# Engine order given by the kernel's own step planner, second-layer weights prepared behind the first batch's heads, transform tables in four transfers

## The chip, the cores and the metric

One Trainium2 chip, one of its cores. The metric is device time of one execution in microseconds (us). The engines are named as the profile names them: PE (TensorE matmul), PEld (its weight loads), DVE (VectorE), ACT (ScalarE), POOL (GpSimd) and SP (SyncE, which here only issues transfers).

## The reference

Attention over 8 batches x 8 heads (576 positions, 64 channels a head, block-causal mask), then a Fourier mixing of each batch, a normalization and a feed-forward layer with residual:

```python
scores = np.where(mask, scale * np.matmul(q, k.transpose(0, 1, 3, 2)), -1000000000.0)
attn = softmax(scores)
x = np.matmul(attn, v)                      # per head, then heads side by side: (8, 576, 512)
u = x + np.real(fft(fft(x, axis=1), axis=2))
un = (u - mean(u)) / np.sqrt(var(u) + 1e-06)
out = u + np.maximum(un @ w_ch1, 0.0) @ w_ch2     # 512 -> 2048 -> 512
```

The two weight matrices arrive as float64, 8.4 MB each.

## The kernel before, in words

The work is cut into small steps. Each step is a `Step` (line 137): a function that records instructions, its cost on PE, a chain of costs on the other engines (D for DVE, A for ACT, G for POOL, Q for SP), the steps it comes after, and a place in the sequence. Lanes yield steps in order: the loads of a head (`head_lane`), its split into a leading part and a rest (`prepare_lane`: `lead` on ACT L293, `rest` on DVE L308 and POOL L310, with two copies L301/L302), the values (`v_lane`, L323 to L340), the row maxima (`max_part`, L388 to L394), their transposed shift (`shift`, L403, and the small copy `lead<-mt`, L405), the scores with two exponentials and a difference (`scores`, ACT L434/L435, POOL L436), the products with the values (`values`, PE into `av`, DVE L471 to L474) and, once per batch, the transform (`fourier_steps`: `mirror`, `folded`, two stages of matmuls, then `normalized_steps`).

The main loop at the end of the kernel walks a model of time. At each turn it picks the step that is ready first, records all of its instructions at once (`step.emit()` in `issue`) and books its chain on queues of the other engines. The feed-forward layer of 256 rows (a "filler", `feed_steps`; 18 of them in all) is taken where no lane is ready. PE keeps the order in which the steps are recorded (`keep_in_program_order`, lines 194 and 197). The order on DVE, ACT, POOL and SP is not given by the kernel: the framework's scheduler sorts those instructions by a time model of its own.

The weights are a side lane, `weight_lane`. Every float64 pair is turned into float32 by three DVE operations over 128x1024 words (`weight_single`, L836 to L838) and one ACT square that sums the magnitude (L839); this is done for 14 pairs of 128-row blocks and 4 single blocks, the first layer's 8 pairs, then the second layer's 6 pairs and 4 singles. Then each of the 32 blocks is scaled and split into two f16 parts (`weight_parts`: ACT L863 and L866 with POOL L867 for the first layer, ACT L863 and DVE L869 for the second). The loads go out on SP's queue (L826), up to three ahead. Heads of the second batch start only when all 18 loads are converted ("w32"). The tables of the transform (2606 KB) come in one transfer on POOL's queue after head 4 (L910).

## Time and profile before

| | us |
|---|---|
| median of 3 runs | 1315.61 (1313.72 to 1317.63) |
| the profiled execution, its own time | 1315.5 |
| its span in the trace | 1313.7 |
| PE busy | 1184.2 |
| DVE busy | 671.9 |
| ACT busy | 548.5 |
| POOL busy | 530.0 |

In the lines of the profile `out<-in` names the tile written and the tiles read, `x14` the number of instructions, and L836 the line of the kernel. A row that groups instructions gives busy time and the mean of one in ns, then the idle time of the engine just before them and what ended it. A row of a window gives the busy us of each engine in that stretch, the clock that PE was granted (1.00 is full), and the share of the transfer engines. "SPq" and "ACTq" are transfers being issued by that engine. A tile's PSUM buffer shows as ps, h or acc whichever ring it was taken from, so those names alone do not tell the step.

### The profile page before, as it was taken

How to read it: one execution, taken by the hardware profiler on the slowest of the kernel's cores; microseconds unless marked ns; L12 is line 12 of the kernel's file. 1: busy time of each engine (PE TensorE's matmuls, PEld its weight loads, DVE VectorE, ACT ScalarE, POOL GpSimd, SP SyncE). 2: the span in 40 equal slices, each digit the busy share in tenths (PEclk: the TensorE clock that was granted, in tenths of full speed). 3: DMA queues.
4: the chain of work that ended last, by engine and by line, in shares of the span. 5: the costliest groups of instructions: out<-in, count | busy, mean ns of one | idle time of the engine just before them, and what ended most of it. 6: DMA issues, size and time to landing. Idle time of an engine off the chain costs nothing.

```text
span 1313.7 us, 25264 instructions
## 1 busy us (share of the span) xinstructions
PE 1184.2 (90%) x10068; PEld 886.7 (67%) x10068; DVE 671.9 (51%) x1440; ACT 548.5 (42%) x1137; POOL 530.0 (40%) x578
## 2 busy tenths in 40 slices
PE   3464469999898999999999999999899999999998
PEld 2363357777676777677777777777677767767665
DVE  6983776445645564655546544746372432412211
ACT  3569355545354444444545354544543112111110
POOL 4668143444544553455443645436442500300000
PEclk9955679999699999999999999999999999999999
DMA  9756213232223223322242133223211000000000
GB/s 280 230 175 177 93 29 77 84 106 64 61 65 92 76 50 90 93 76 51 80 115 75 44 96 104 73 70 86 79 30 49 30 12 17 22 1 17 16 17 17
DMA packets 55941, 99.10 MB, mean 75 GB/s; under 512 B 7709, under 2 KB 26605, under 8 KB 55696
## 3 DMA queue, kind: packets, MB, share of 16 engines
q1 hardware_dynamic: 52176, 87.56, 23.5%
q0 software_dynamic: 2288, 7.54, 1.9%
q10 hardware_dynamic: 1360, 2.38, 0.6%
q8 instruction: 80, 1.31, 0.4%
q14 instruction: 37, 0.30, 0.1%
HBM read 58.46 MB, written 18.87 MB: 59 GB/s over the span
## 4 chain that ended last, share of the span: by engine, by line
PE 76%; DVE 10%; ACT 4%; DMA 3%; POOL 3%; issue 3%; SPq 0%; ACTq 0%; DVEq 0%; POOLq 0%
PE h L194 27%; PE acc L194 26%; PE ps L194 16%; PE av L194 5%; POOL pl L436 2%; PE ps L197 1%; DVE M L392 1%; DVE W L837 1%; DMA W<-in_moe_w_ch_dram 1%; DVE rest L308 1%; DVE W L838 1%; ACT lead L293 1%; DVE tmp L549 1%; DMA U<-xd,rows 1%; DVE W L836 1%
## 5 line engine op out<-in xcount | busy, mean ns | idle before, releaser
L194 PE MATMUL h<-uh,W 128*128 128x256 f16 x2304 | 434.9, 275 | 0.0
L436 POOL TENSOR_TENSOR pl<-p,ph 128x288 f16<-128x288 f32 (+1 forms) x256 | 257.9, 1017 | 395.8 <-ACT p L435 249.6
L194 PEld LDWEIGHTS <-W 128*128 128x128 f16 x3456 | 325.8, 99 | 64.3 <-issue 4.0
L194 PE MATMUL acc<-W,gh 128*128 128x512 f16 x1152 | 347.2, 383 | 0.0
L194 PE MATMUL h<-ul,W 128*128 128x256 f16 x1152 | 316.2, 274 | 0.0
L194 PE MATMUL acc<-W,gl 128*128 128x512 f16 x576 | 220.1, 382 | 0.4 <-DVE gl L750 0.4
L750 DVE SCALAR_TENSOR_TENSOR gl<-h,gh 128x512 f16<-128x512 f32 x144 | 98.9, 687 | 227.3 <-ACT gh L749 227.2
L194 PE MATMUL ps<-lead 72*128 72x64 f32 (+9 forms) x700 | 196.5, 342 | 12.5 <-ACT lead L293 6.8
L749 ACT ACTIVATE gh<-h 128x512 f16<-128x512 f32 x144 | 85.9, 596 | 268.4 <-PE h L194 267.7
L434 ACT ACTIVATE ph<-ps 128x512 f16<-128x512 f32 (+1 forms) x229 | 116.0, 507 | 121.0 <-PE ps L194 119.7
L194 PEld LDWEIGHTS <-gh 128*128 128x128 f16 x1152 | 101.0, 99 | 87.8 <-issue 8.2
L392 DVE TENSOR_REDUCE M<-ps 128x1 f32<-128x320 f32 (+3 forms) x235 | 120.5, 527 | 47.9 <-PE ps L194 46.7
L194 PE MATMUL av<-VH,pl 128*128 128x65 f16 x960 | 115.9, 200 | 31.7 <-POOL pl L436 31.5
L194 PEld LDWEIGHTS ps<-lead 72*128 72x128 f32 (+1 forms) x700 | 125.6, 201 | 20.8 <-ACT lead L293 6.8
L194 PEld LDWEIGHTS <-ph 128*128 128x128 f16 x1920 | 113.0, 103 | 34.1 <-DVE x L474 8.4
L310 POOL TENSOR_TENSOR rest<-raw,lead 64x576 fp32r<-64x576 f32 x64 | 116.2, 1816 | 23.3 <-ACT lead L293 18.5
L194 PE MATMUL av<-VH,ph 128*128 128x65 f16 x960 | 118.1, 202 | 8.2 <-DVE x L474 7.6
L194 PE MATMUL ps<-rest 128*128 128x64 f32 (+2 forms) x345 | 121.6, 360 | 1.8 <-DVE M L392 1.1
L435 ACT ACTIVATE p<-ps 128x512 f32<-128x512 f32 (+1 forms) x229 | 115.9, 506 | 10.2 <-POOL pl L436 10.1
L194 PE MATMUL av<-VL,ph 128*128 128x64 f16 x960 | 117.3, 200 | 0.0
L194 PEld LDWEIGHTS <-pl 128*128 128x128 f16 x960 | 93.6, 102 | 34.9 <-POOL pl L436 34.8
L308 DVE TENSOR_TENSOR rest<-raw,lead 64x576 fp32r<-64x576 f32 x64 | 60.0, 938 | 88.4 <-ACT lead L293 88.3
(171 smaller groups left out, 1376.7 us busy)
## 6 DMA issues: line engine op xcount, KB each, us to landing
raw<-in_qk_dram SPq DMA_DIRECT2D x64, 288.0 KB
rest<-lead SPq DMA_DIRECT2D x112, 144.0 KB
W<-in_moe_w_ch_dram SPq DMA_DIRECT2D x14, 1024.0 KB
V<-in_v_dram SPq DMA_DIRECT2D x32, 320.0 KB
xd<-x SPq DMA_DIRECT2D x32, 256.0 KB
out_dram<-u SPq DMA_DIRECT2D x32, 256.0 KB
u<-xd SPq DMA_DIRECT2D x8, 512.0 KB
dft<-in_c_dft_dram POOLq DMA_DIRECT2D x1, 2606.0 KB, 11.3
```

The source lines that it names most:

```text
L194: return tc.keep_in_program_order(nc.tensor.matmul(*args, **kw))
L197: return tc.keep_in_program_order(nc.tensor.transpose(*args, **kw))
L293: nc.scalar.copy(LEAD[h % NB][0:D, 64:], raws[h])
L308: nc.vector.tensor_tensor(x0[0:D, 0:S], raw[:, 0:S], x1[0:D, 64:64 + S], op=ALU.subtract)
L310: nc.gpsimd.tensor_tensor(x0[D:P, S:], raw[:, S:], x1[0:D, 64 + S:], op=ALU.subtract)
L392: nc.vector.tensor_reduce(m[:, j:j + 1], t[:, at - hi:at], axis=AX.X, op=ALU.max)
L434: nc.scalar.activation(ph[:, at:at + w], t[:, 0:w], AF.Exp, scale=0.125)
L435: nc.scalar.activation(p32[:, 0:w], t[:, 0:w], AF.Exp, scale=0.125)
L436: nc.gpsimd.tensor_tensor(pl[:, at:at + w], p32[:, 0:w], ph[:, at:at + w], op=ALU.subtract)
L549: nc.vector.tensor_tensor(e[0:r], X[c][0:r], U[c][0:r], op=op)
L749: nc.scalar.activation(gh, t, AF.Relu)
L750: nc.vector.scalar_tensor_tensor(gl, t, 0.0, gh, op0=ALU.max, op1=ALU.subtract)
```

## The change

1. **Order.** A class `Ordered` wraps DVE, ACT, POOL and SP so that all their instructions keep the order in which the kernel records them. A step no longer records everything at once: its function has become a generator with a `yield` behind the part of each engine. `issue` books the chain, notes a start time for each part, and `give` records the parts whose planned start has come before the next PE step is recorded. The planner's model gains queues for the port that DVE and POOL share (K) and for transfers (M), and rings for three scratch tiles.
2. **Weights.** The loads form a lane of their own and go out on ACT's queue; the first two also wait for the first V and the first two heads. Two further lanes prepare the layers: the second layer's conversions come after head 7's values and after the first layer's scale. Heads of the second batch wait for the last f16 part of the first layer instead of for all 18 conversions. The first layer's f16 parts start after its scale step, which stood on PE behind the scores of head 5 and now stands inside the first batch's transform.
3. **Tables.** Four transfers instead of one, after heads 1, 2, 4 and 5, each behind a one-element DVE operation.
4. **Smaller edits.** For the first batch the copies of `lead_copies` and `shift` move from ACT's queue to SP's, as for the other batches before. The last maximum (L394) becomes a `tensor_scalar` with the second operand as a per-partition scalar. In the first batch's transform the 12 additions of stage 2 move from DVE to POOL, as in the other batches. Several `need` conditions (recorded before) become `after` conditions (done before, in the model).

The core of the diff:

```diff
+class Ordered:
+    def __getattr__(self, name):
+        f = getattr(self.engine, name)
+        def given(*args, **kw):
+            x = f(*args, **kw)
+            return self.tc.keep_in_program_order(x) if hasattr(x, "ins") else x
+        return given
...
+    def give(t):
+        soon = sorted((x for x in pending if x[0] <= t), key=lambda x: x[:2])
+        pending[:] = [x for x in pending if x[0] > t]
+        for _, _, parts in soon:
+            next(parts, None)
...
-            nc.vector.tensor_tensor(m[:, 4:5], m[:, 4:5], m[:, 5:6], op=ALU.max)
+            vector.tensor_scalar(m[:, 4:5], m[:, 4:5], m[:, 5:6], None, op0=ALU.max)
...
-            engine = nc.vector if b == 0 else nc.gpsimd
+            engine = gpsimd
...
-            nc.sync.dma_start(raw(x).rearrange("p (j n) -> p j n", j=n), weight(i, n))
+        if x < 2:
+            vector.tensor_copy(raw(x)[0:1, 0:1].bitcast(F32), raws[x][0:1, 0:1])
+            yield
+        scalar.dma_start(raw(x).rearrange("p (j n) -> p j n", j=n), weight(i, n))
...
+                    (("WL", x),) + ((("WS", x - 1),) if x else ()) + ((("scale", 0), ('V', 7, 4)) if w else ()), ("WS", x),
...
-        nc.vector.tensor_scalar(dft[0:1, 0:1], DEN[0][0:1, 0:1], 0.0, None, op0=ALU.mult)
-        nc.gpsimd.dma_start(dft, c_dft)
+        vector.tensor_scalar(dft[0:1, lo:lo + 1], DEN[i % 2][0:1, 0:1], 0.0, None, op0=ALU.mult)
+        yield
+        gpsimd.dma_start(dft[:, lo:hi], c_dft[:, lo:hi])
...
-            if x is not None and may(x) and (i == len(lanes) - 1 or x.place < H or "w32" in done)
+            if x is not None and may(x) and (i == len(lanes) - 1 or x.place < H or ('w', 15) in done)
```

What this does to the order is shown at three places. In the changed kernel every instruction of DVE, ACT, POOL and SP carries line 194, that of `given`.

DVE between the end of head 0 and the end of head 1 (`x<-av` is a head's last DVE operation, `W<-W` the conversion of weights, `M` the maxima, `rest` the split of a coming head). Before, the first 12 of 30 rows:

```order
L474 TENSOR_TENSOR x<-av,rec 128x5x64
L836 TENSOR_SCALAR W<-W 128x1024
L337 TENSOR_SCALAR vacc<-pw 128x1
L837 SCALAR_TENSOR_TENSOR W<-W 128x1024
L838 SCALAR_TENSOR_TENSOR W<-W 128x1024
L392 TENSOR_REDUCE M_91<-ps 128x1 x2
L836 TENSOR_SCALAR W<-W 128x1024
L392 TENSOR_REDUCE M_91<-h 128x1
L340 SCALAR_TENSOR_TENSOR VL_97<-V,vacc,VH_95 128x640
L837 SCALAR_TENSOR_TENSOR W<-W 128x1024
L308 TENSOR_TENSOR rest_88<-raw,lead_85 64x576
L394 TENSOR_TENSOR M_91<-M_91 128x1
```

Now, all rows of that stretch:

```order
L194 TENSOR_TENSOR x<-av,rec 128x5x64
L194 TENSOR_REDUCE M_91<-h 128x2
L194 TENSOR_REDUCE M_91<-h 128x1
L194 TENSOR_TENSOR rest_87<-raw,lead_84 64x576
L194 SCALAR_TENSOR_TENSOR VL_97<-V,vacc,VH_95 128x640
L194 TENSOR_REDUCE M_91<-acc 128x1 x2
L194 TENSOR_REDUCE M_91<-ps 128x1
L194 TENSOR_SCALAR M_91<-M_91 128x1
L194 TENSOR_TENSOR rest_88<-raw,lead_85 64x576
L194 TENSOR_SCALAR DEN_93<-av,vacc 128x5
L194 RECIPROCAL rec<-DEN_93 128x5
L194 TENSOR_TENSOR x<-av,rec 128x5x64
```

No conversion stands there any more. Counted over the whole order, all 14 pairs stood ahead of head 7's `x<-av` before and 6 do now; the other 8 stand between it and the first normalization of the transform, and the 4 singles, which stood among the transform's first operations, come behind that normalization.

ACT in the first batch's transform (`ZT`, `fs` and `zs` are the transform's tiles, `W<-W,wst` and `un<-W,wst` the f16 parts of the first layer, `left,ul<-W` the square of a converted pair). Now:

```order
L194 CAST ZT<-ps 2x290
L194 ACTIVATE left,ul<-W 128x1024
L194 DMA W<-in_moe_w_ch_dram 128x2x1024
L194 CAST fs_1294<-tmp 32x256 x2
L194 CAST fs_1298<-tmp 128x256
L194 CAST fs_1312<-tmp 128x256
L194 ACTIVATE W<-W,wst 128x512
L194 ACTIVATE un<-W,wst 128x512
L194 CAST zs_1335<-h 128x288
L194 ACTIVATE W<-W,wst 128x512
```

Before, those parts began among the exponentials (`ph`, `p`) of head 6:

```order
L435 ACTIVATE p_899<-ps 128x512
L434 ACTIVATE ph_960<-h 128x288
L863 ACTIVATE W<-W,wst 128x512
L866 ACTIVATE un<-W,wst 128x512
L863 ACTIVATE W<-W,wst 128x512
L435 ACTIVATE p_965<-h 128x288
L866 ACTIVATE un<-W,wst 128x512
L434 ACTIVATE ph_960<-h 128x288
```

So the first layer's f16 parts move from the last two heads of the batch to the middle of its transform, and a load of weights stands in ACT's order ahead of casts.

SP at the start of the program (`raw` a head's q and k, `V` the values of two heads, `rest<-lead` and `lead<-mt` the copies that a head waits for). Before:

```order
L290 DMA raw<-in_qk_dram 64x1152
L314 DMA V<-in_v_dram 128x640
L290 DMA raw<-in_qk_dram 64x1152
L826 DMA W<-in_moe_w_ch_dram 128x2x1024 x4
L290 DMA raw<-in_qk_dram 64x1152 x2
L826 DMA W<-in_moe_w_ch_dram 128x2x1024
L314 DMA V<-in_v_dram 128x640
```

Now:

```order
L194 DMA raw<-in_qk_dram 64x1152
L194 DMA V<-in_v_dram 128x640
L194 DMA raw<-in_qk_dram 64x1152
L194 DMA rest_87<-lead_84 64x576 x2
L194 DMA raw<-in_qk_dram 64x1152
L194 DMA rest_88<-lead_85 64x576 x2
L194 DMA lead_84<-mt 1x5x128
```

The weights are gone from SP's order; the copies of the first batch have come into it.

More of the change, by code (lines that the diff above doesn't have):

```diff
@@ L247, in tile_attn_fourier_ffn @@
     now = 0.0
-    queues = {x: Queue() for x in "DAGQ"}
+    queues = {x: Queue() for x in "DAGQKM"}
     done = {}
@@ L259, in ready, with book @@
         return max(r, min(rings[x][0] for x in lent)) if step.bank else r
+    def book(engine, t, cost):
+        used = [queues[x] for x in {"X": "DK", "G": "GK", "P": "G"}.get(engine, engine)]
+        while True:
+            at = max(x.fit(t, cost) for x in used)
+            if at <= t:
+                return max(x.book(t, cost) for x in used)
+            t = at
+    pending = []
+    issued = [0]
     def issue(step):
@@ L263, in issue @@
         t = max(now, ready(step))
+        if step.cost:
+            give(t)
         if step.cost:
@@ L268, in issue @@
         free = None
+        starts = []
         for engine, cost in step.chain:
@@ L500, in max_lane @@
                 )
[L501 removed]
+            yield Step(lambda: shift(h), 0.12, ("A0.26", "B", "Q0.6", "M0.05", "L1.6"), (("M", h),), ("X", h), True, place=h - 0.6)
     def value_lane():
@@ L934, in tile_attn_fourier_ffn @@
         until = max(now, min(until, default=now))
-        if side is not None and may(side) and ready(side) <= until:
-            engine, cost = side.chain[0] if side.chain else (None, 0.0)
+        first = min((heads[i].place for i in able), default=H) >= H
+        for w, side in enumerate(sides):
+            if side is None or not may(side) or ready(side) > until:
+                continue
+            engine, cost = next((x for x in side.chain if x[0] in "DAGQKXP"), (None, 0.0))
             at = max(now, ready(side))
-            ahead = queues[engine].fit(at, cost) - at if engine else 0.0
-            first = min((heads[i].place for i in able), default=H) >= H
-            if ahead <= AHEAD[engine == "D" and first] or at + ahead + cost + FREE <= until:
+            ahead = queues[{"X": "D", "P": "G"}.get(engine, engine)].fit(at, cost) - at if engine else 0.0
+            if ahead <= AHEAD[engine in ("D", "X") and first] or at + ahead + cost + FREE <= until:
                 issue(side)
-                side = next(weights, None)
-                continue
+                sides[w] = next(weights[w], None)
+                break
+        else:
+            w = None
+        if w is not None:
+            continue
         feed = filler is not None and may(filler)
@@ L952, in tile_attn_fourier_ffn @@
             i = min(able, key=lambda i: ready(heads[i]))
-        elif side is not None:
-            issue(side)
-            side = next(weights, None)
+        elif any(sides):
+            w = min((w for w, x in enumerate(sides) if x is not None and may(x)), key=lambda w: ready(sides[w]))
+            issue(sides[w])
+            sides[w] = next(weights[w], None)
+            continue
+        elif pending:
+            give(pending[0][0])
             continue
```

385 lines of the change are left out of this document (230 added, 155 removed).

## The prediction, made before the changed kernel was run

> **What bounds the kernel now.** I read the page first, then windows by stage, then who PE waits for, and last the chain of waits in the stage where PE stands idle. The page gives the span, the engines, PE in 40 slices of 32.8 us and the clock granted to it:
>
> ```profile
> span 1313.7 us, 25264 instructions
> PE   3464469999898999999999999999899999999998
> PEclk9955679999699999999999999999999999999999
> ```
>
> PE is full from the seventh slice on; the first six, about 200 us, are not. There the 25 us windows show (PE, PEld, DVE, ACT, POOL, clock, transfer share):
>
> ```profile
> 0.00:25.00 25.00, 5.02 (x16) 3.83 (x16) 14.46 (x39) 7.29 (x10) 7.35 (x25) 1.00 0.91 267
> 25.00:50.00 25.00, 14.39 (x84) 11.96 (x84) 25.00 (x34) 14.53 (x32) 17.66 (x8) 1.00 0.83 270
> ...
> 125.00:150.00 25.00, 2.93 (x17) 1.92 (x15) 13.61 (x29) 10.88 (x23) 10.90 (x12) 0.50 0.44 155
> ...
> 325.00:350.00 25.00, 18.83 (x127) 14.14 (x126) 20.35 (x49) 8.17 (x19) 19.28 (x28) 0.70 0.27 67
> ```
>
> DVE is full at 25 to 50 us while PE does 14 of 25: the conversion of weights holds the heads back. At 125 to 150 nothing is full: that is a chain. I cut the start at three events, which the chain of waits names (start, us): head 7's last DVE operation, the wait for weights, the first fold of the transform, and the end of the first normalization; and, far down, two equal points of consecutive feed-forward layers:
>
> ```profile
> 4.57 14.90 DMA W<-in_moe_w_ch_dram
> ...
> 126.11 0.50 DVE x L474
> ...
> 129.84 6.87 DMA u<-in_moe_w_ch_dram
> ...
> 141.38 1.28 DVE tmp L549 x2
> ...
> 171.39 0.56 DVE un L694
> ...
> 1045.49 5.24 PE h L194 x48
> ...
> 1088.05 5.24 PE h L194 x48
> ```
>
> So the heads of batch 0 end at 126.6, its transform is normalized at 172, and a feed-forward layer costs PE 42.6 us. The same three stages as windows:
>
> ```profile
> 126.60:172.00 45.40, 17.08 (x90) 13.25 (x90) 29.55 (x70) 18.91 (x43) 17.17 (x22) 0.65 0.29 95
> 0.00:126.60 126.60, 62.31 (x531) 53.60 (x531) 94.75 (x171) 78.20 (x152) 82.32 (x77) 0.80 0.71 218
> 172.00:266.00 94.00, 89.48 (x816) 68.44 (x817) 57.08 (x124) 51.76 (x102) 38.43 (x37) 0.91 0.24 65
> ```
>
> PE idles 64.3 us in the first, 28.3 in the second, 4.5 in the third. Beyond 200 us and up to the last heads it waits little, and for these above all:
>
> ```profile
> PE av L194 <- POOL pl L436: 15.1, 13, 2.1
> PE ps L194 <- DVE M L392: 4.2, 8, 1.1
> PE ps L197 <- DVE M L394: 3.9, 4, 1.5
> ```
>
> PE's own work hardly changes, so what the change can win lies nearly all ahead of 200 us. The sum is made against the profiled execution's 1315.5 us, 0.1 below the median of the three runs; 0.3%, 3.9 us, is about what a measurement of this kernel can tell from no change.
>
> **Stage 1, the heads of batch 0.** The conversions cost, by form:
>
> ```profile
> L838 DVE SCALAR_TENSOR_TENSOR W<-W 128x1024 int32<-128x1024 int32 x14 | 19.2, 1368 | 0.1
> L837 DVE SCALAR_TENSOR_TENSOR W<-W 128x1024 int32<-128x1024 int32 x14 | 18.5, 1330 | 0.1
> L836 DVE TENSOR_SCALAR W<-W 128x1024 int32<-128x1024 int32 x14 | 11.9, 851 | 0.0
> ```
>
> One pair is 1368 + 1330 + 851 = 3549 ns. Eight of 14 pairs leave the stage: 8 x 3.55 = 28.4 us of DVE. Of its 126.6 us DVE is busy 94.75, so 66.4 remain beside 31.9 idle. What can become late next? ACT's 78.2 us lose eight squares and the f16 parts that ran among the last heads:
>
> ```profile
> L839 ACT ACTIVATE left<-W 128x1024 f16<-128x1024 f32 x14 | 14.8, 1054 | 6.2 <-DVE W L838 6.1
> L866 ACT ACTIVATE un<-W,wst 128x512 f32<-128x512 f32 x16 | 11.2, 709 | 7.2 <-PE h L197 6.3 <-POOL W L867 0.8
> ```
>
> Eight squares are 8.4 us; most of the 16 `un` parts (11.2 us) and of their equally long partners go too. POOL's per-head work, by the page,
>
> ```profile
> L436 POOL TENSOR_TENSOR pl<-p,ph 128x288 f16<-128x288 f32 (+1 forms) x256 | 257.9, 1017 | 395.8 <-ACT p L435 249.6
> L310 POOL TENSOR_TENSOR rest<-raw,lead 64x576 fp32r<-64x576 f32 x64 | 116.2, 1816 | 23.3 <-ACT lead L293 18.5
> ```
>
> is (257.9 + 116.2) / 64 = 5.8 us a head, 47 for eight; with the splits of coming heads and the weights' differences POOL was busy 82.3 in the stage, and the differences leave it too: no bound, but the next to become one. A second gain is at the start. The first shift copy on ACT's queue was held until a 1 MB weight load landed at 19.47, with the values' scaling behind it on ACT, and DVE waited for that:
>
> ```profile
> 19.57 1.27 ACTq L405 DMA_DIRECT2D lead<-mt  x1
> 20.88 0.83 ACT L339 ACTIVATE VH<-V,vacc 128x640 f16<-128x640 f32 x1 [7.88 <-issue]
> 21.75 0.88 DVE L340 SCALAR_TENSOR_TENSOR VL<-V,vacc,VH 128x640 f16<-128x640 f32 x1 [4.43 <-ACT VH L339]
> ```
>
> Now the copy is on SP's queue with no load ahead of it there, and the scaling stands ahead of it on ACT; I count DVE's 4.4 us. Stage 1: 126.6 - 28.4 - 4.4 = 93.8. Ends: 76, if DVE's idle falls to about the 10 us of the first window; 112, if latencies in the heads eat half.
>
> A rule of the Trainium skill speaks against those 4.4 us: "DMA: Bandwidth & Descriptors", section "Issuing engines are not separate DMA queues", says that transfers from SP, ACT and POOL run on the same engines and interleave, and that issuing from several saves only issue time. The transfer share of 0.91 in the first window agrees that they are full. By the rule the term is 0, and my sum would be 4.4 higher.
>
> SP gets the batch's 24 copies and loses 18 loads. Behind a copy that waits for ACT stands the next head's load; I count nothing, since that load is for a head two places on, and up to the 4.4 us above if that cover fails. The tables' three more issues on POOL I count at nothing either: POOL's differences are waited for by PE, but it had 44 us free in the stage. Bare, they cost a few us at most, as a `pl` of 1 us each.
>
> **Stage 2, the transform of batch 0.** DVE gets the eight pairs, 28.4 us. It loses the four singles, which also were what the transform waited behind:
>
> ```profile
> L836 DVE TENSOR_SCALAR W<-u 128x512 int32<-128x512 int32 x4 | 1.7, 420 | 10.1 <-DMA u<-in_moe_w_ch_dram 10.1
> L837 DVE SCALAR_TENSOR_TENSOR W<-u,W 128x512 int32<-128x512 int32 x4 | 2.8, 689 | 0.1
> L838 DVE SCALAR_TENSOR_TENSOR W<-u,W 128x512 int32<-128x512 int32 x4 | 2.8, 688 | 0.1
> L634 DVE TENSOR_TENSOR u<-u,add 128x255 f32<-128x255 f32 x2 | 0.8, 394 | 0.0
> ```
>
> The singles are 7.3 us; the 12 additions that move to POOL about 12 x 0.4 = 4.8. So DVE's 29.55 become 45.9. Of its 15.9 us idle, 10.1 were the wait for the last load; the batch's own reload keeps perhaps 4 of them, the rest may be filled. 45.9 plus about 4 is 50 against 45.4 now: +4.6. Ends: -6, if the pairs fill only idle time and the fold starts earlier; +16, if none is hidden. The additions take POOL longer than DVE, and ACT gets the parts that left stage 1; both run beside DVE's 50 us. If they don't, they are in the upper end.
>
> **Stage 3, up to a full PE.** The second layer's four singles and 16 parts come behind the first normalization, so the first feed-forward layer's second half starts later, and heads of batch 1 fill PE instead. PE lost only 4.5 us of idle here before, plus 9% of clock. I take 0; ends: -6 (that idle gone and some clock), +10 (singles and parts, 7.3 and about 12 us of DVE, half bare).
>
> **Beyond.** The maximum's last operation (L394) had a spread that a per-partition scalar form of the same size doesn't show:
>
> ```profile
> L394 DVE TENSOR_TENSOR M<-M x64: 131/153/1346, 10.9 to 983.3; 128x1 f32<-128x1 f32 x64
> L334 DVE TENSOR_SCALAR pw<-vacc x32: 106/147/155, 12.2 to 960.0; 128x1 int32<-128x1 int32 x32
> ```
>
> PE waited 3.9 us for it beyond 200; I count half, -2. The order given on all engines I count at 0 there, with both signs open (rivals).
>
> **Sum:** -28.4 - 4.4 + 4.6 + 0 - 2 = -30.2; 1315.5 - 30.2 = 1285.3. I say 1285, own range 1270 to 1300.
>
> **Rivals.** *ACT blocked by its loads (slower).* All 18 loads now stand in ACT's strict order. One that waits for its landing place or for an earlier transfer holds the casts and exponentials behind it, and PE and POOL wait for those. The 7.88 us before L339 shows that it happens. It decides at 30.2 / 18 = 1.7 us blocked per load; at 2.4 the loss is 43 and the time 1328. For it: 0.91 share at the start. Against: ACT keeps some 55 us of work (78.2 - 8.4 - about 15) in a stage of 94, so most blocking falls into idle time. 0.10.
>
> *A strict order stalls at the turns between batches.* At 325 to 350 PE lost 6.2 us idle and 18.8 x 0.30 = 5.6 of clock. Two more such turns of the remaining six give 1285 + 24 = 1309, three 1320. For: DVE and POOL are at 20 and 19 of 25 there, and nothing can now slip past a late instruction. Against: the trace before has one bad turn only, in an order that also was fixed before the run. 0.12.
>
> *The start's transfers stay slow.* At a share of 0.91 the copies get their turn among 1 MB loads wherever they were issued, and the 4.4 us come back: 1285.3 + 4.4 = 1290. This is the Trainium skill's rule above. 0.12.
>
> *The given order also fills the later gaps.* PE's later waits for `pl`, L392 and L394 sum to 23.2; all but the counted 2 gone is 1264. For: the planner now books the port that POOL and DVE share. Against: `pl` waits hang on POOL's own length. 0.14.
>
> *That the order isn't kept* is ruled out by the rows of the changed kernel's order.
>
> The forecast keeps 0.52. Below 1311.6 lie it, the third and fourth rival and 0.05 of the second: faster 0.83. Within 0.3%: 0.05 of the second. Slower: the first and 0.02 of the second, 0.12. The range leaves out ACT blocked, the turns' upper 0.07 and a little below: 1256 (the fourth rival, 1264, less 8 of the 10.6 by which stage 2's lower end is shorter) to 1310.
>
> **What would show it.** Right: head 7's `x` ends at 84 to 104, the first normalization at 134 to 154, DVE busy over 40 us between them; no 10 us wait ahead of the fold; PE full from about 170. Wrong: ACT idle behind load issues of over 1.7 us each; PE idle beyond 200 us above 35; or the second half of the first feed-forward layer waiting for weights by over 10.

## The result, and the profile after

The changed kernel takes 1300.21 us (median of 4 runs, 1299.14 to 1301.94) against 1314.66 for the kernel before in the same session (1312.98 to 1317.63): ratio 0.9889, 95% interval [0.9867, 0.9911]. The forecast was 1285, so the sign was right, 1300 lies in the range, and 14.4 us came of the forecast 30. The profiled execution took 1299.14 us, with a span of 1297.0. Its page, span, PE and clock in 40 slices of 32.4 us:

```profile
span 1297.0 us, 25139 instructions
PE   6764168999899999899999999999999999999998
PEclk9999567999899999989999999999999999999999
```

The first two slices are fuller than before (67 for 34), the fifth is emptier (1 for 4); the third, fourth and sixth are as before. All instructions of DVE, ACT, POOL and SP carry line L194 now, that of the helper that keeps the order, so they are told apart by tile and shape. The three stages of the prediction, with the second cut at the end of the second `un` (the normalized rows), as windows (PE, PEld, DVE, ACT, POOL, clock, transfer share, GB/s):

```profile
0.00:91.20 91.20, 69.78 (x529) 60.92 (x529) 68.76 (x146) 54.36 (x110) 59.45 (x58) 1.00 0.74 207
91.20:173.70 82.50, 27.06 (x143) 20.49 (x143) 53.10 (x74) 43.10 (x79) 53.00 (x54) 0.77 0.40 129
173.70:266.00 92.30, 82.78 (x706) 63.44 (x707) 65.01 (x139) 51.28 (x105) 35.31 (x35) 0.84 0.33 87
```

Head 7's `x` ends at 91.2 (forecast 93.8), the second `un` of the first normalization at 173.7 (forecast 144). The prediction's 172.0 was the end of the first `un`; the second ended at 173.1 before:

```profile
172.53 0.52 DVE L694 TENSOR_SCALAR un<-u,ag 128x512 f32<-128x512 f32 x1
```

From the second `un` to the end it is 1123.3 us, 1140.6 before. By these cuts the change is -35.4, +36.0 and -17.3.

The cuts mark events of the transform, not what PE lost. Since PE's work is nearly the same, windows of 100 us, and one from 300 to 1000, say better where the time lies. The kernel before:

```profile
0.00:100.00 100.00, 49.37 (x400) 42.72 (x400) 83.73 (x147) 54.13 (x107) 57.93 (x57) 0.86 0.74 228
100.00:200.00 100.00, 54.98 (x422) 44.07 (x421) 63.07 (x139) 61.04 (x121) 52.51 (x54) 0.64 0.33 98
200.00:300.00 100.00, 96.83 (x900) 72.09 (x899) 52.41 (x123) 49.28 (x103) 42.80 (x40) 0.98 0.31 84
300.00:1000.00 700.00, 673.79 (x6178) 514.02 (x6176) 388.38 (x881) 336.54 (x717) 345.04 (x376) 0.98 0.28 75
```

And after:

```profile
0.00:100.00 100.00, 69.78 (x529) 60.92 (x529) 71.81 (x148) 55.51 (x112) 60.88 (x60) 1.00 0.76 219
100.00:200.00 100.00, 43.91 (x270) 33.55 (x270) 69.57 (x111) 51.93 (x100) 60.79 (x64) 0.73 0.37 109
200.00:300.00 100.00, 96.94 (x871) 74.52 (x871) 63.46 (x138) 59.38 (x125) 43.40 (x43) 0.93 0.31 82
300.00:1000.00 700.00, 687.01 (x6377) 529.40 (x6377) 407.80 (x892) 336.02 (x720) 334.41 (x375) 0.99 0.28 75
```

PE's idle time, window less busy: -20.4 us in the first 100, +11.1 in the second, nothing in the third, -13.2 from 300 to 1000, and -0.4 behind it: 129.5 becomes 106.5. Its busy time went from 1184.2 to 1190.5. Together that is the span's 16.7. So of 20.4 us gained up to 100, 11.1 went back up to 200; 13.6 came from the later batches, to which the forecast had given 2; and PE's own work, which the forecast took as unchanged, took 6.3 back.

What DVE waited for in the transform after (85 to 180 us; us in total, times, longest):

```profile
DVE W L194 <- DMA W<-in_moe_w_ch_dram: 11.3, 2, 10.0
DVE tmp L194 <- DMA U<-xd,rows: 9.4, 1, 9.4
DVE dif L194 <- PE acc L216: 4.3, 1, 4.3
```

The last addition of the transform, after which its statistics could be taken, ends on POOL at 145.6:

```profile
144.89 0.72 POOL L194 TENSOR_TENSOR u<-u,dif 128x255 f32<-128x255 f32 x1
```

DVE's own rows from 161 us on, and the issue of the load that the first of them waits for:

```profile
161.06 1.28 DVE L194 TENSOR_SCALAR W<-W 128x1024 int32<-128x1024 int32 x1 [10.03 <-DMA W<-in_moe_w_ch_dram]
162.38 4.16 DVE L194 SCALAR_TENSOR_TENSOR W<-W 128x1024 int32<-128x1024 int32 x2
166.47 1.70 DVE L194 TENSOR_TENSOR rest<-raw,lead 64x576 fp32r<-64x576 f32 x1
168.09 0.93 DVE L194 TENSOR_REDUCE M<-ps 128x2 f32<-128x128 f32 x3
168.96 0.67 DVE L194 BATCH_NORM_STATS2 st<-u 128x6 f32<-128x512 f32 x1
```

```profile
156.19 0.37 ACTq L194 DMA_DIRECT2D W<-in_moe_w_ch_dram  x1
```

DVE stood 10 us in front of a conversion whose weights had not landed, with the statistics (`st<-u`) queued behind it: they start 23.4 us after the last addition. The load went out late: its landing place in the kernel's list is that of the pair before it. DVE ended that pair's conversion at 151.0; the load stood in ACT's order behind its square and went out 5.2 us later, and the conversion started 4.9 us after that.

### The profile page after: what moved, and what is told of

Read it like the earlier page. It is cut to its first block, busy times and chain, and to the rows that moved or that the text cites. A ratio compares the mean times of both kernels' runs of the same rounds, so it can differ in the third digit from the quotient of the medians.

```text
span 1297.0 us, 25139 instructions
## 1 busy us (share of the span) xinstructions
PE 1190.5 (92%) x10068; PEld 899.2 (69%) x10068; DVE 695.1 (54%) x1433; ACT 547.3 (42%) x1137; POOL 529.8 (41%) x593
## 4 chain that ended last, share of the span: by engine, by line
PE 80%; DVE 8%; POOL 4%; DMA 3%; issue 2%; ACT 2%; SPq 0%; DVEq 0%; ACTq 0%; POOLq 0%
PE acc L216 28%; PE h L216 28%; PE ps L216 17%; PE av L216 6%; DVE W L194 2%; PE ps L219 2%; DVE M L194 2%; POOL u L194 1%; POOL pl L194 1%; DVE tmp L194 1%; DMA W<-in_moe_w_ch_dram 1%; DMA xd<-x 1%; POOL ag L194 1%; DVE un L194 1%; DMA raw<-in_qk_dram 1%
## 5 line engine op out<-in xcount | busy, mean ns | idle before, releaser
L194 POOL TENSOR_TENSOR pl<-p,ph 128x288 f16<-128x288 f32 (+1 forms) x256 | 260.4, 1028 | 346.9 <-ACT p L194 185.7
L194 DVE TENSOR_REDUCE M<-ps 128x1 f32<-128x192 f32 (+4 forms) x294 | 131.0, 481 | 174.8 <-PE ps L216 174.6
L216 PE MATMUL ps<-lead 72*128 72x64 f32 (+9 forms) x700 | 200.1, 348 | 24.8 <-ACT lead L194 18.2
L194 ACT ACTIVATE gh<-h 128x512 f16<-128x512 f32 x144 | 85.8, 596 | 321.3 <-PE h L216 320.9
L216 PE MATMUL acc<-W,gl 128*128 128x512 f16 x576 | 218.8, 380 | 1.2 <-DVE gl L194 1.2
L194 DVE SCALAR_TENSOR_TENSOR gl<-h,gh 128x512 f16<-128x512 f32 x144 | 98.6, 686 | 200.2 <-ACT gh L194 199.8
L194 ACT ACTIVATE ph<-ps 128x288 f16<-128x288 f32 (+1 forms) x232 | 116.6, 505 | 169.4 <-PE ps L216 168.6
L216 PEld LDWEIGHTS <-gh 128*128 128x128 f16 x1152 | 100.7, 99 | 83.6 <-issue 4.3
L216 PEld LDWEIGHTS ps<-lead 72*128 72x128 f32 (+1 forms) x700 | 128.2, 204 | 34.0 <-ACT lead L194 18.6
L216 PE MATMUL ps<-rest 128*128 128x288 f32 (+3 forms) x347 | 124.5, 366 | 1.9 <-ACT p L194 1.3
L194 ACT ACTIVATE p<-ps 128x288 f32<-128x288 f32 (+1 forms) x232 | 116.3, 504 | 1.4 <-POOL pl L194 1.3
L216 PEld LDWEIGHTS <-gl 128*128 128x128 f16 x576 | 56.4, 98 | 70.3 <-DVE gl L194 2.7
L194 POOL TENSOR_TENSOR rest<-raw,lead 64x576 fp32r<-64x576 f32 x64 | 96.2, 1504 | 17.5 <-ACT lead L194 11.9
```

The source lines that it names most:

```text
L194: x = f(*args, **kw)
L216: return tc.keep_in_program_order(nc.tensor.matmul(*args, **kw))
```

## The experiments

Theory A: the heads gain because eight pairs leave them, and the transform gives it back because conversions, their loads and the first layer's late parts stand ahead of the normalization. Rival B: POOL, with the additions and the parts, makes the transform long. Rival C: the reload of the heads' output does. Rival D: the gain is the kept order, wherever the weights stand.

All 18 runs, in one table. Ratio: to the kernel before in the same call, with its interval. "Head 7", "norm" and "2nd half": us at which head 7's `x` ends, the second `un` ends, and the first matmul of a feed-forward layer's second half starts. Idle and busy are PE's, idle up to 200 and from 300 to 1000 us, of the profiled execution. "Plan": whether the planner's decisions are those of the kernel after. These moments are of one execution each. In seven kernels the orders of all engines are the same up to head 7's `x` (after, additions on DVE with and without the plan kept, no hold, parts on DVE with and without the gate, nudge), and it ends there between 90.9 and 94.2; a difference of 3 us in such a moment tells nothing.

| kernel | us | ratio | plan | head 7 | norm | 2nd half | idle to 200 | idle 300-1000 | busy |
|---|---|---|---|---|---|---|---|---|---|
| before | 1314.7 | 1 | - | 126.6 | 173.1 | 195.4 | 95.7 | 26.2 | 1184.2 |
| after | 1300.2 | .9889 [.9867, .9911] | - | 91.2 | 173.7 | 213.8 | 86.3 | 13.0 | 1190.5 |
| order not kept | 1328.0 | 1.0109 [1.0087, 1.0131] | same | 121.7 | 188.7 | 223.4 | 101.1 | 25.9 | 1188.7 |
| whole steps | 1425.8 | 1.0844 [1.0822, 1.0867] | same | 100.6 | 191.5 | 241.5 | 100.5 | 67.0 | 1231.3 |
| two-input maximum | 1306.6 | .9937 [.9920, .9953] | same | 93.6 | 176.1 | 216.7 | 89.9 | 16.6 | 1192.4 |
| copies on ACT | 1308.4 | .9961 [.9947, .9975] | same | 95.1 | 178.7 | 219.7 | 93.6 | 15.6 | 1188.0 |
| additions on DVE, plan kept | 1298.3 | .9874 [.9848, .9900] | same | 92.0 | 171.4 | 212.9 | 85.4 | 12.4 | 1192.5 |
| additions on DVE | 1291.9 | .9827 [.9804, .9850] | new | 94.2 | 170.7 | 218.7 | 78.2 | 6.8 | 1193.1 |
| no hold | 1296.3 | .9855 [.9828, .9882] | new | 92.7 | 174.5 | 211.5 | 83.6 | 9.4 | 1191.3 |
| second layer later | 1319.3 | 1.0035 [1.0021, 1.0050] | new | 93.7 | 162.2 | 268.1 | 77.6 | 8.5 | 1212.6 |
| more pairs in the heads | 1286.0 | .9785 [.9761, .9809] | new | 106.8 | 194.2 | 214.2 | 74.6 | 7.1 | 1194.1 |
| loads unchained | 1286.3 | .9788 [.9762, .9815] | new | 101.7 | 180.4 | 218.6 | 71.5 | 5.6 | 1190.9 |
| additions and early loads | 1274.8 | .9697 [.9681, .9713] | new | 93.6 | 165.7 | 214.0 | 73.9 | 3.2 | 1184.3 |
| one table | 1294.5 | .9858 [.9841, .9875] | new | 95.8 | 173.6 | 218.8 | 81.9 | 4.8 | 1192.3 |
| early loads, no hold | 1284.5 | .9774 [.9755, .9794] | new | 99.1 | 165.8 | 212.0 | 84.8 | 9.4 | 1184.8 |
| parts on DVE | 1304.6 | .9909 [.9890, .9928] | new | 92.8 | 173.9 | 244.0 | 74.0 | 6.0 | 1210.0 |
| parts on DVE, no gate | 1312.6 | .9980 [.9970, .9989] | new | 90.9 | 149.2 | 227.8 | 80.8 | 12.0 | 1202.6 |
| early loads, one table | 1302.3 | .9915 [.9902, .9928] | new | 97.0 | 178.9 | 222.6 | 77.6 | 15.5 | 1190.5 |
| early loads, parts on DVE | 1299.7 | .9882 [.9866, .9899] | new | 95.0 | 164.6 | 243.7 | 63.6 | 8.8 | 1205.4 |
| nudge from batch 2 on | 1301.7 | .9900 [.9875, .9926] | late new | 93.9 | 176.7 | 218.3 | 86.8 | 14.4 | 1190.2 |

### What the kept order is worth, and its grain

*Order not kept.* The helper returns the instruction without pinning it:

```diff
-            return self.tc.keep_in_program_order(x) if hasattr(x, "ins") else x
+            return x
```

> The kernel after, but DVE, ACT, POOL and SP no longer keep the order of the steps; the planner, the second layer's late conversions, the split tables and the additions on POOL stay. Kernel after: 1300.2 us, 91.2 us up to head 7's x (stage 1), 82.5 us from there to the first normalization (stage 2). Theory A (stage 2 was lost because the strict order of DVE and ACT puts conversions that wait for their loads ahead of the transform): the 10 us wait in front of a conversion no longer holds the statistics; stage 2 falls to 55 to 70 and the time to 1275 to 1290. Theory B (POOL is too full, by additions and first-layer parts): stage 2 stays within 8 us of 82. Theory D (what was won came from the given order in the later batches, not from the pairs that left the heads): PE's waits beyond 200 us go back from about 17 to about 29 and the time to 1308 to 1315.

1328.0 us, slower than the kernel before. Its windows up to 100 and from 300 to 1000 us:

```profile
0.00:100.00 100.00, 48.58 (x363) 42.29 (x364) 81.31 (x146) 51.43 (x101) 51.97 (x56) 0.81 0.80 245
300.00:1000.00 700.00, 674.14 (x6171) 515.49 (x6172) 403.74 (x900) 334.28 (x712) 348.74 (x374) 0.99 0.28 75
```

PE's idle is back at the old values in both. All 14 pairs of conversions begin ahead of head 7's `x`, 6 in the kernel after, though the plan holds eight back in both. Who PE waits for between 300 and 1000 us here:

```profile
PE av L216 <- POOL pl L194: 12.6, 13, 2.1
PE ps L216 <- DVE M L194: 7.1, 6, 2.4
```

And in the kernel after:

```profile
PE av L216 <- POOL pl L194: 1.8, 3, 1.0
PE ps L216 <- DVE M L194: 0.9, 2, 0.6
```

With the same plan, the kept order is worth 28 us, some 15 of it up to 200 us and 13 behind. D holds for the 13. For the 15 this run can't tell D from A: without the kept order the eight pairs are back ahead of head 7.

*Whole steps.* Each step's instructions are given out at once, the order kept:

```diff
-        if step.cost:
-            next(parts, None)
-        for at in starts:
-            pending.append((at, len(pending) + 1000000 * issued[0], parts))
-        issued[0] += 1
+        for _ in parts:
+            pass
```

> The kernel after, but each step's instructions are given out at once, as in the kernel before, not part by part; DVE, ACT, POOL and SP still keep the order. Without any kept order the kernel after took 1328.0 us, with it 1300.2. Theory D1 (a kept order alone is the gain, whatever its grain): 1296 to 1304. Theory D2 (it is the grain: given out whole, an engine stands in front of a step's late part while the next step's first part is ready): 1315 or more, head 7's x later than 105 us, and PE's waits beyond 200 us above 30.

1425.8: a kept order of whole steps costs 111 us against the kernel before. ACT's rows at a turn between batches show how:

```profile
602.55 0.84 ACT L194 CAST fs<-tmp 32x257 fp32r<-32x257 f32 x2 [2.00 <-DVE tmp L194]
...
605.49 0.41 ACT L194 CAST fs<-tmp 128x257 fp32r<-128x257 f32 x1 [1.67 <-DVE tmp L194]
607.45 0.41 ACT L194 CAST fs<-tmp 128x257 fp32r<-128x257 f32 x1 [1.55 <-DVE tmp L194]
607.76 0.59 ACT L194 ACTIVATE gh<-h 128x512 f16<-128x512 f32 x1
608.25 0.40 ACT L194 ACTIVATE ph<-ps 128x288 f16<-128x288 f32 x1
```

The three folds wait for DVE one after the other, with a `gh` and a `ph` queued behind them; PE stands idle for 5.4 us there, up to 609.0, and is released by an exponential behind that `ph`. The rival "a strict order stalls at the turns between batches" is what this kernel does; giving the parts out at their planned starts avoids it here.

### The heads

*No hold.* The second layer's conversions aren't held back until the first layer's scale and head 7:

```diff
-  ((("WS", x - 1),) if x else ()) + ((("scale", 0), ('V', 7, 4)) if w else ()), ("WS", x),
+  ((("WS", x - 1),) if x else ()), ("WS", x),
```

> The kernel after, but the second layer's conversions aren't held back until the first layer's scale and head 7: they may stand among batch 0's heads, as in the kernel before. Theory A: stage 1 goes from 91 back to 115 to 125 us and stage 2 from 82 to 45 to 55, so that the sum moves by -10 to +5; time 1290 to 1306. If the pairs that left were worth what the prediction counted (28 us, with nothing given back), the time goes up by 20 or more, to 1320. Theory D (the gain is from the given order alone): 1300 plus or minus 4, with PE's waits beyond 200 us still about 17.

Head 7's `x` ends at 92.7, and 1296.3 is not told apart from the kernel after. Up to head 7's `x` the orders of all engines are those of the kernel after: the hold keeps nothing out of the heads that the loads' pace in the plan and the kept order don't keep out by themselves. Theory A's expectation for this run fell.

*More pairs in the heads.* No hold, unchained loads at a smaller planned cost, four in flight, more room:

```diff
-AHEAD = (1.5, 6.0)
-FLIGHT = 3
+AHEAD = (20.0, 20.0)
+FLIGHT = 4
...
-  f"M{1.8 * n}"
+  f"M{0.1 * n}"
```

> The kernel after, but the planner is told to bring weights early: no hold on the second layer, a load doesn't wait for the one before it, a load costs the shared transfers 0.1 in place of 1.8 a half MB, four in flight, more room ahead. The order is still kept. In DVE's order 10 pairs of conversions then stand ahead of head 7's x, where 6 stood. Theory A (a pair in the heads costs its DVE time, 3.55 us): head 7's x comes at 91.2 + 4 x 3.55 = 105 or later. Theory D (a kept order is what shortened the heads, and DVE's 22 us idle there takes the pairs in): head 7's x before 97. If the first layer's late pairs and parts made stage 2 long, the first normalization comes before 165 (173.7 now) and the time is 1285 to 1295 either way; if not, 1300 or more.

The trace has 11 pairs ahead of head 7's `x`, not the 10 named. The heads as a window, and that `x`:

```profile
0.00:106.77 106.77, 70.30 (x531) 60.42 (x531) 91.01 (x166) 62.83 (x126) 67.21 (x65) 0.90 0.76 228
```

DVE's busy time grew by 91.0 - 68.8 = 22.2 us and the stage by 15.6, that is 3.1 for each of the five pairs (2.5 to 3.8 with 3 us of uncertainty in the moment), or 0.70 us for a us of DVE. So a pair in the heads costs about what the prediction gave it (3.55). Yet the kernel, with the rest laid out anew, is 14 us faster than the kernel after: pairs in the heads need not make it slower.

*Copies on ACT.* Batch 0's copies are issued on ACT's queue, at the same places of the plan:

```diff
-        sync.dma_start(dst.bitcast(F32), mt.bitcast(F32))
+        (scalar if h < H else sync).dma_start(dst.bitcast(F32), mt.bitcast(F32))
```

and the same for the two halves' copies.

> The kernel after, but batch 0's 24 copies (the heads' halves and the shift) are issued on ACT's queue again, at the same places of the plan, not on SP's. The prediction's term: the copies behind ACT's weight loads cost DVE 4.4 us at the start, so 1303 to 1307 and head 0's x 4 us later than 28.8. If it doesn't matter which queue issues them, since all use the same transfer engines: 1298 to 1302. If 24 issues of 0.5 to 1.2 us on ACT hold its exponentials, some 20 us of issue in the heads: 1310 or more.

The whole takes 8.2 us more. Head 7's `x` is 3.9 us later, which is 0.9 behind the latest of the seven kernels above. ACT's rows at the first shift copy here:

```profile
12.31 0.39 ACTq L194 DMA_DIRECT2D W<-in_moe_w_ch_dram  x1
12.79 1.42 ACTq L194 DMA_DIRECT2D lead<-mt  x1
...
19.17 0.41 ACT L194 ACTIVATE ph<-h 128x288 f16<-128x288 f32 x1 [3.13 <-PE h L216]
```

In the kernel after the copy is issued at 11.51, on SP's queue, and the first `ph` starts at 16.05:

```profile
11.51 0.85 SPq L194 DMA_DIRECT2D lead<-mt  x1
```

and ACT's row of that `ph`:

```profile
16.05 0.41 ACT L194 ACTIVATE ph<-h 128x288 f16<-128x288 f32 x1 [0.27 <-PE h L216]
```

From issue to use it is 4.5 us on SP's queue here and 6.4 on ACT's, behind a 1 MB load issued 0.5 us earlier. But on SP's queue, in the seven kernels above, the same copy takes 4.5 to 6.8 us. So this copy shows no more than the 1.3 us of later issue, which the rule of the Trainium skill that the prediction weighed ("DMA: Bandwidth & Descriptors", section "Issuing engines are not separate DMA queues") allows. Whether the 8.2 us are ACT's time for 24 issues or the queue stays open.

*Two-input maximum.*

```diff
-  vector.tensor_scalar(m[:, 4:5], m[:, 4:5], m[:, 5:6], None, op0=ALU.max)
+  vector.tensor_tensor(m[:, 4:5], m[:, 4:5], m[:, 5:6], op=ALU.max)
```

> The kernel after with one instruction per head as in the kernel before: the maximum's last operation takes two tensors (131 to 1346 ns in the kernel before) instead of a tensor and a scalar for each partition (about 0.2 us). The plan and every order stay. The prediction's 2 us for it: 1302 to 1304. If its spread came from where it stood and not from its form: 1298.5 to 1301.5, and its longest is under 300 ns.

1306.6: with the plan and every order kept, the form is worth 6.4 us, three times the 2 that were counted. Its durations here (minimum, median, maximum in ns):

```profile
L194 DVE TENSOR_TENSOR M<-M x64: 159/160/1353, 9.9 to 975.5; 128x1 f32<-128x1 f32 x64
```

and in the kernel after:

```profile
L194 DVE TENSOR_SCALAR M<-M x64: 212/214/216, 9.8 to 966.4; 128x1 f32<-128x1 f32 x64
```

The scalar form is longer in the median and has no tail.

*One table.* One transfer in place of four, behind head 1 (before the change it stood behind head 4), with its planned cost:

```diff
-        lo, hi = ends[i], ends[i + 1]
+        lo, hi = 0, c_dft.shape[1]
-        for i in range(4):
+        for i in range(1):
...
-  "M2.3"
+  "M9.2"
```

> The kernel after, but the transform's tables come in one transfer of 2.6 MB behind head 1, as in the kernel before, not in four. In the plan one more pair of conversions then falls ahead of head 7's x (7, not 6). If the four transfers are worth nothing, as the prediction counted: 1297 to 1303. If one transfer of 2.6 MB holds up the heads' own (the kernel before had a transfer share of 0.91 at the start): head 7's x later than 97 and 1304 or more. If the extra pair in the heads shortens the transform as unchaining the loads did (1286.3): 1292 to 1296.

1294.5, which the intervals don't tell apart from the kernel after. The same edit on the fastest kernel gave the opposite sign:

> The fastest kernel (1274.8: additions on DVE in batch 0, loads planned earlier), with the tables in one transfer of 2.6 MB behind head 1. Here the pairs of conversions keep their places against the heads, unlike in the earlier try with one table (1294.5 against 1300.2). If four transfers are worth something: 1277 or more, and the heads between the second and the fourth lose 2 or more. If the transfer's cut is worth nothing and the earlier gain was the extra pair: 1273 to 1277. If one transfer is better in itself: 1272 or less.

1302.3, 27 us more. PE's idle there grew by 12 us between 300 and 1000, where the orders are laid out anew. What the cut of the tables is worth stays open.

### The transform

*Additions on DVE*, as before the change, told to the planner:

```diff
-            engine = gpsimd
+            engine = vector if b == 0 else gpsimd
-  ("D0.86", "B", "G3.0")
+  ("D0.86", "B", "X1.66" if b == 0 else "G3.0")
```

> The kernel after, but batch 0's twelve additions of its transform are on DVE again, as in the kernel before. Theory B (POOL full, the chain of additions from 130.8 to 145.6 us on it sets the end of stage 2): additions take 5 us instead of 15, the first normalization comes 10 or more earlier, time 1286 to 1291. Theory A (the statistics stand in DVE's order behind a conversion that waited 10 us for its load until 161): stage 2 moves by less than 4 us, time 1296 to 1303.

1291.9 seemed to speak for B. The same without the second edit, so that the rest of the plan stays:

> The kernel after with batch 0's twelve additions on DVE, but with the planner's costs left as they are, so that the order of every engine is that of the kernel after, but for these twelve. (The earlier try, 1291.9, told the planner too, and it laid out the whole rest of the program anew.) Theory B, POOL's additions lengthen stage 2: the first normalization 4 to 10 earlier and 1290 to 1295. If the earlier gain of 8.4 us was the new layout behind batch 0: 1298 to 1302.

1298.3, not told apart from the kernel after; the normalization comes 2.3 us earlier, within the spread of such moments, and DVE still stands in front of the late load:

```profile
159.04 1.05 DVE L194 TENSOR_SCALAR W<-W 128x1024 int32<-128x1024 int32 x1 [8.43 <-DMA W<-in_moe_w_ch_dram]
```

So the additions on POOL are not what makes the transform long, and some 6 of the 8.4 us came with the new layout.

*Second layer later.* Its conversions wait for the first normalization:

```diff
-  ((("scale", 0), ('V', 7, 4)) if w else ())
+  ((("scale", 0), ("n", 1, 1)) if w else ())
```

> The kernel after, but the second layer's conversions wait for the first normalization instead of head 7's last values: none stands ahead of batch 0's transform. Theory A: the 10 us wait for a load and some 8 x 3 us of conversions leave stage 2; it falls from 82 to 52 to 62 us, and the next stage grows by 5 to 10, as the second half of the first feed-forward layer waits for weights; time 1280 to 1290. Theory B (POOL's parts of the first layer's weights and the additions set the end, 121 to 168 us of full POOL): stage 2 stays above 74, time 1296 to 1306. Theory C (the reload of the heads' output, 5.65 us instead of 2.29, and the fold's start at 103.7): the fold still starts 12 us behind head 7's x.

The normalization comes 11.5 us earlier, as A has it in direction, but at 162 and not at 146 to 156; and the kernel is 19 us slower. The second half's matmuls, first and last start:

```profile
L216 PE MATMUL acc<-W,gh x1152: 376/379/650, 268.1 to 1314.3; 128*128 128x512 f16 x192
```

and the third window:

```profile
200.00:300.00 100.00, 84.54 (x679) 68.21 (x679) 75.33 (x148) 62.88 (x135) 59.35 (x52) 0.68 0.42 117
```

In the kernel after that half starts at 213.8:

```profile
L216 PE MATMUL acc<-W,gh x1152: 376/379/634, 213.8 to 1292.3; 128*128 128x512 f16 x192
```

PE's idle in total is the same as in the kernel after (106.3 us); its busy time is 22 us longer, at a granted clock of 0.68 in the third window in place of 0.93.

*Parts on DVE.* The first layer's sixteen parts use one cast on ACT and one subtraction on DVE:

```diff
-        if w == 0:
-            scaled = work.tile([P, DM], F32, name="un", bufs=2)
-            scalar.activation(scaled, t, AF.Copy, scale=sc)
-            yield
-            gpsimd.tensor_tensor(W[:, i, 1], scaled, W[:, i, 0], op=ALU.subtract)
-            yield
-            return
```

> The kernel after, but the first layer's sixteen weight parts are made as the second layer's are: one cast on ACT and one subtraction on DVE (about 0.75 us each by the second layer's rows), instead of two casts on ACT and a subtraction on POOL (1.4 us each, 22.5 us of POOL in stage 2). Theory B (POOL is what makes stage 2 long): 16 x 1.4 us leave POOL, the first normalization comes 10 or more before 173.7, time 1284 to 1291. Theory E (the late first-layer weights as such: their eighth pair stands behind head 7, and parts and gate follow it): some 5 us from POOL's and ACT's parts, DVE takes 12 more, time 1293 to 1302.

The normalization doesn't move (173.9). PE's waits for POOL between 100 and 200 us, in the kernel after

```profile
PE av L216 <- POOL pl L194: 16.8, 5, 13.7
```

are fewer here, the largest row being

```profile
PE av L216 <- POOL ul L194: 6.6, 2, 4.4
```

and PE's idle up to 200 is 12 us shorter; but the second half starts 30 us later, PE is busy 19.5 us longer in all, and the time isn't told apart from the kernel after. B holds for a wait of PE, not for the length of the stage, and not for the time.

*No gate.* The change had added a condition to the first normalization, the first layer's last part. In this kernel, with the parts on DVE, it is taken away:

```diff
-  keys + ((("w", NF - 1),) if me == 1 else ())
+  keys
```

> The kernel before this one in the list (first layer's parts on ACT and DVE), and the first normalization no longer waits in the plan for the first layer's last part. Theory E': the gate keeps the normalization behind parts that end at 163; without it it comes 10 or more earlier, but the first feed-forward layer still waits for the parts, so the time falls by 2 to 6 against the kernel without this edit. If additions and the strict order of DVE set the normalization, nothing moves (within 2 us).

The normalization comes at 149.2, 24.7 us earlier by this line and the order that it brings; the time rises by 8 us. So in this kernel the gate is what holds the normalization, and an earlier normalization doesn't make it faster. In the kernel after the gate was not taken away alone; there the statistics start 23.4 us after the last addition, which fits.

*Loads unchained.* A load no longer waits in the plan for the one before it:

```diff
-  ... for y in {x - FLIGHT, *same} if y >= 0) + ((("WL", x - 1),) if x else ())
+  ... for y in {x - FLIGHT, *same} if y >= 0)
```

> The kernel after, with one condition less: a weight load no longer waits in the plan for the load before it to land. 8 pairs of conversions, all of the first layer, then stand ahead of head 7's x or right behind it, 6 before. Theory A: head 7's x at 98 us, the first layer's parts start near 105 instead of 120, the first normalization is 8 to 12 earlier, time 1288 to 1294. If stage 2 hangs on POOL's additions and on the reload: the normalization moves by less than 4, time 1297 to 1304.

1286.3, faster than the kernel after by an interval that doesn't touch its. The first layer's parts (ACT's second cast, first and last start) run from 91.8 to 141.3:

```profile
L194 ACT ACTIVATE un<-W,wst x16: 705/711/722, 91.8 to 141.3; 128x512 f32<-128x512 f32 x16
```

in the kernel after from 120.7 to 161.1:

```profile
L194 ACT ACTIVATE un<-W,wst x16: 704/707/722, 120.7 to 161.1; 128x512 f32<-128x512 f32 x16
```

Yet the normalization came later, not earlier: near the time that A named (1288 to 1294), but not for its reason. PE was idle 15 us less up to 200: two heads of batch 1 ended ahead of the normalization, and PE did 406 matmuls in the second window, 270 in the kernel after.

```profile
100.00:200.00 100.00, 62.31 (x406) 50.98 (x404) 79.15 (x124) 57.59 (x116) 70.52 (x73) 0.58 0.37 109
```

*Additions and early loads*, `FLIGHT = 4` and a planned cost of 0.5 for 1.8 besides:

> The kernel after with two things together: batch 0's twelve additions on DVE (that alone took 8.4 us off, 1291.9), and weight loads planned earlier (not behind the load before, 0.5 in place of 1.8 a half MB, four in flight), so that 7 pairs stand ahead of head 6's x and the eighth ahead of the transform. If both shorten stage 2 by causes of their own: 1278 to 1286. If they take the same time away, or the earlier loads crowd the heads' transfers: 1290 to 1296.

1274.8, the fastest, 1.9% under the kernel after by the ratios. Its stages up to 300 us:

```profile
0.00:100.00 100.00, 66.29 (x531) 58.18 (x531) 85.07 (x161) 63.14 (x126) 64.16 (x65) 0.76 0.83 242
100.00:200.00 100.00, 59.78 (x442) 48.21 (x442) 82.33 (x140) 56.70 (x118) 54.84 (x60) 0.67 0.36 108
200.00:300.00 100.00, 94.90 (x840) 73.68 (x838) 70.71 (x148) 60.57 (x126) 53.20 (x54) 0.94 0.29 80
```

DVE has 85 and 82 of 100 us to do where it had 72 and 70. Two more edits on top of it:

> The fastest kernel so far (1274.8: additions on DVE in batch 0, weight loads planned earlier) with the second layer's conversions no longer held behind the first layer's scale and head 7. The first eight pairs stay in the heads. If holding the second layer back is worth anything in itself: 1279 or more. If the kept order and the loads' pace alone decide, as in the kernel after (1296.3 without the hold, 1300.2 with it): 1270 to 1277.

1284.5, 10 us more. The layouts differ as well, so these 10 us are not put down to the hold alone.

> The fastest kernel (1274.8) with the first layer's parts on ACT and DVE, none on POOL. If POOL still bounds the transform there: 1264 to 1270. If DVE is the bound once the additions are back on it: 12 us more of DVE, half of it bare, 1277 to 1283. In the plan the normalization falls behind head 9's x instead of head 8's, which speaks for the second.

1299.7: the least idle up to 200 us of all (63.6), a second half at 243.7, and 21 us more of PE's busy time.

### What a new layout is worth by itself

A change of one planned cost from batch 2 on, with no instruction changed:

```diff
-  ("D0.95",) + (("Q1.2",) if h % 2 else ())
+  ("D0.95" if h < 16 else "D1.0",) + (("Q1.2",) if h % 2 else ())
```

> The kernel after with one planned cost of DVE, the heads' last step, 1.00 in place of 0.95 us from batch 2 on. No instruction is added, moved to another engine or taken away; the orders are the same up to about the first normalizations and laid out anew behind them. If single layouts are worth little: 1298 to 1302, and PE's idle between 300 and 1000 us stays at 13 within 3. If a layout is a draw of several us: outside 1296 to 1304, and then a difference of 10 us between two kernels whose plans differ tells nothing of the edit alone.

1301.7, and 14.4 us of idle between 300 and 1000: the new layout shows no effect (1.5 us, within the intervals). But the kernels marked "new" in the table are laid out anew from the heads or from the first transform on, with 3.2 to 15.5 us of idle between 300 and 1000. Differences of 10 us between two of them are not put down to their edit here.

## Why the prediction was right or wrong

- **Stage 1, -32.8: right** in size (-35.4) and in the main in mechanism. By the run with more pairs a pair in the heads costs 3.1 us, so the eight are some 25 of the 35.4; the other 10, for which 4.4 were counted, lie in the start and the order, and no run separates the two. That the diff's hold moves the pairs was wrong: without it the same pairs stay out; without the kept order they come back in despite it.
- **The 4.4 us of the start: they came, but not shown to be the queue.** DVE no longer waits at the scaling, and head 0's `x` ends at 28.8 for 48.4, so the rival "the start's transfers stay slow" falls. The first shift copy was issued at 19.57 before and at 11.51 after; from ACT's queue in the kept order at 12.79, and from SP's queue without the kept order at 22.91. So the order brought it forward. The copies on SP's queue are worth 8.2 us of the whole, by a cause that is open.
- **Stage 2, +4.6: this step failed,** with +36.0. It was summed from DVE's work, "45.9 plus about 4" us of idle. DVE was busy 53.1 and idle 29.4: the stage was not DVE's work but a chain, which had been ready for the normalization at 145.6, near the forecast 144, and then waited. Two things were left out. One is a condition that the diff adds in one line, the normalization behind the first layer's last part (24.7 us by the run without it, in the kernel with the parts on DVE). The other is that two of the eight pairs that leave the heads are the first layer's, so that its sixteen parts end on ACT at 161.8, where 14 of them ended by 131 before. The kept order then put the statistics behind a conversion that stood 10 us in front of its load. How the 36 us divide among the three was not measured. That the sixteen parts' work "runs beside" was true for the engines and false for the chain.
- **What of it reached the time:** not 36 but 11 us of PE's idle between 100 and 200. The normalization's moment is no measure of the end: without the gate it came 24.7 us earlier and the kernel was slower.
- **Stage 3, 0: near, in part by luck.** From the second `un` to 266 us PE idled 9.5 us for 4.4 before, inside the named ends; from 200 to 300 its idle is unchanged. The second half of the first layer starts 18 us later than before (213.8 for 195.4), as the text expected in direction, and PE stayed full. But in the four kernels in which that half started at 227.8 or later with the parts given out as planned, PE was busy 12 to 22 us longer than in the kernel after.
- **Beyond, -2:** PE's idle there fell by 13.6. The rival "the given order also fills later gaps" was right in kind and got more than half of its 23 us; the run without the kept order shows it. The maximum's form was mis-sized as well, 6.4 us for 2.
- **The wait ahead of the fold,** forecast to shrink to 4 us, was 9.4: the load it hung on was replaced by the reload. No run changed the reload by itself, but from head 7's `x` to the first fold it is 12.5 us, 14.8 before, so the 36 us lie behind the fold and rival C is not what made the stage longer.
- The rival "ACT blocked by its loads" gave 1328, which did not come; no run moved the loads off ACT, so their share is not known. That PE's own work hardly changes was a term put at nothing: its busy time grew by 6.3 us, and why is open.

## What to carry to other kernels

In this kernel a kept order paid only with every engine's parts standing in it at their own planned starts; the same plan given out step by step was 126 us slower. When work leaves a stage, follow it to the next thing that waits for it, conditions added in the same diff included, and price that chain, not the busy time of the engine that does it. A change to a planner's rules changes the whole program behind it: try the edit with the plan left as it is, and take the idle and the busy time of the busiest engine together, not the moment of an event, as the measure. Compare such moments only after looking at how far they move between kernels whose order up to there is the same.

## What the runs showed of the hardware that was not expected

- PE's busy time for the same 10068 matmuls differs by up to 28 us between kernels, whole steps left out. In four kernels whose second half started at 227.8 to 268.1, with a granted clock of 0.68 to 0.82 between 200 and 300 us, PE was busy 1202.6 to 1212.6 us; in all others but that of whole steps the half started by 223.4 and PE was busy 1184.2 to 1194.1, at 0.86 to 0.98. The same matmul (`av<-VH,ph`) took 243 ns in the median between 200 and 300 us with the second layer later, 195 in the kernel after. With the parts on DVE PE idled 11.8 us less in all than in the kernel after, was busy 19.5 longer, and the time didn't fall. The Trainium skill's page "TensorE: Matmul & The Clock Gate", section "Part 1: The HAM clock gate", says that the clock follows how busy PE has been; between 200 and 300 us the rows agree in direction (0.68 at 84.5 of 100 us busy, 0.93 at 96.9). The granted clock alone doesn't give the price: in the first 100 us the kernel after was granted 1.00 and that with parts on DVE and no gate 0.65, in the same order up to head 7, and PE's 529 matmuls there took 69.8 and 66.6 us.
- A two-input DVE operation on one column took 160 ns in the median and up to 1353; with one input as a scalar for each partition, 212 to 216 ns at all 64 places. The form that is longer in the median made the kernel 6.4 us faster. The Trainium skill's page "SBUF — State Buffer", section "Who interferes with whom", says that a DVE instruction with two inputs in SBUF contends with a POOL instruction that reads SBUF; the tail that goes with the second tensor input agrees, and no run here took POOL's work away to show it alone.
